# Two edits at the head of a fused DeltaNet and SwiGLU kernel: the first square roots move from GpSimd to VectorE, and the gate of the first weight loads moves behind a second pair of norms

## The chip, the cores and the metric

The kernel runs on one core of one Trainium2 chip. The time is that of the device, in microseconds (us), and the figure compared is the median of several runs. TensorE (PE) multiplies matrices and loads its weights in separate records (PEld), VectorE (DVE) and ScalarE (ACT) work on vectors, GpSimd (POOL) does some small work and issues a few transfers, and SyncE (SP) does nothing but issue transfers, in order. The instructions of each engine run in the order in which they were written; engines meet through semaphores.

## What is computed

The first half is a DeltaNet attention over 4 batches, 8 heads, 768 steps and 48 channels. The second is a SwiGLU block on 3072 tokens with 384 features and 1536 hidden units.

```python
k_n = k / (np.linalg.norm(k, axis=-1, keepdims=True) + 1e-06)
for t in range(S):
    y[:, :, t] = einsum('bhd,bhde->bhe', q[:, :, t], state)
    v_old = einsum('bhde,bhd->bhe', state, kt)
    state = state + bt[..., None, None] * einsum('bhd,bhe->bhde', kt, vt - v_old)
x = y.transpose(0, 2, 1, 3).reshape(B * S, H * D)
g = x @ w_gate
out = (g / (1 + exp(-g)) * (x @ w_val)) @ w_out
```

The change concerns `np.linalg.norm` of the first 128 steps: its square root.

## The kernel before, in words

The 768 steps are cut into 12 chunks of 64. A chunk holds all 32 pairs of batch and head at once; two chunks make a group, and for each group the recurrence inside a chunk is solved as a triangular system. Chunk by chunk, `advance` (four steps) turns the solved system and the running state into the tokens of the SwiGLU block, `x_ffn`. From then on TensorE does the large products `p_gate` and `p_val` (`gate_val`, L825) and `p_o`, and the attention of later chunks is fitted between them. The order of every engine is written out by hand, since the schedule is a manual one.

The head of the program, before the first `p_gate`, runs so:

- SP issues half of k for chunks 0 and 1 (`load_k`, L119; ACT issues the other half), then half of the beta loads (`load_beta`, L355; POOL issues the other half). Next come the first four pieces of the feed-forward weights (`stage`, L232), q of chunk 0 (`load_q`, L127), k of chunks 2 and 3, weight pieces 4 to 9, v of chunk 0 (`load_v`, L167), q of chunk 1, weight pieces 10 to 16, v of chunk 1, and q of chunk 2. They stand in one queue.
- The first weight piece is written into the buffer `places[0]`, whose first column DVE clears with a `memset` (L1128). The piece overwrites that column, so SP may not issue it before the `memset`. Everything behind it on SP waits too. In the kernel before, the `memset` stands between the norms of chunk 0 and those of chunk 1.
- `norms(c)` squares k on DVE (L331), sums the squares in three reductions (L339), and GpSimd then takes the square root with `pow` and an exponent of 0.5 (L343), 16 values in each partition for each of the two chunks.
- PE transposes k of chunks 0 and 1 (L410), forms the products of k with itself (`first_gram`, L524 and L525), and `first_diag` (L530) copies their diagonal blocks out, half of them by ACT and half by DVE. `first_n` (L364 to L368) adds the epsilon, takes the reciprocal and transposes it; `first_scale` (L543 to L546) scales beta on POOL and the matrix `mb` on DVE; `substitute` (L488, L494) solves the system of 32 columns on DVE in 62 dependent instructions.
- Meanwhile PE, in its order, transposes q of chunk 0 and k of chunks 2 and 3, forms their products (L422), transposes the matrices of the second group (`turned_m`, L566) and q of chunk 1 (L410). Only then does `join_late` for chunk 0 follow (L598, L608), which joins the halves of the solved system. It needs the result of `substitute` through `late_z` (L574, L580) and the ACT copies `d_o` (L591). Its result `zt` is copied by ACT (L616); then come `p_u` (L741), `p_y` (L760), the transposes `p_f` (L805), `x_ffn` (L808) and the first `p_gate` (L825).

The square roots of the later groups (`invert`, L633) stay on GpSimd in both kernels. The tile `n_t[0]` holds the 32 sums, later the norms, of the first group; `first_n` reads it, and ACT reads it in `scale_v_heads` (L374).

Of the kernel before, what the change touches and what calls it, by code (L numbers as in the profile page):

```python
# [8 lines left out]
FP32 = mybir.dt.float32  # L9
U32 = mybir.dt.uint32  # L10
ALU = mybir.AluOpType
# [4 lines left out]
R = 32  # L16
# [4 lines left out]
def kernel(  # L21
# [25 lines left out]
    nc = tc.nc  # L47
# [10 lines left out]
    HH = NB * H  # L58
# [4 lines left out]
    work = ctx.enter_context(tc.tile_pool(name="work", bufs=2))  # L63
# [60 lines left out]
    def load_q(c):  # L124
        for bp in range(NB):
            for b in range(2):
                nc.sync.dma_start(  # L127
                    out=qpad[c % QB][64 * b : 64 * b + 64, bp, :, 0:D],
                    in_=halves(q, c, bp, b).rearrange("h p d -> p h d"),
                )  # L130
# [59 lines left out]
    def words(tile_):  # L190
        return tile_.bitcast(U32)
# [95 lines left out]
    half = const.tile([128, R], FP32, name="half")  # L287
# [7 lines left out]
    for b in range(2):  # L295
        rows = mask_q[64 * b : 64 * b + 64]
        nc.gpsimd.affine_select(
            out=rows,
# [13 lines left out]
    def half_of(x):  # L312
        return slice(64 * x, 64 * x + 64)
# [7 lines left out]
    n_t = {}  # L321

    def new_n(g):

        n_t[g] = work.tile([128, 2, HH], FP32, name="n_t")

    def norms(c):

        ksq = work.tile([128, NB, H, D], FP32, name="ksq", tag="r", bufs=2)
        x = knp[c][:, :, :, 0:D]  # L330
        nc.vector.tensor_tensor(out=ksq, in0=x, in1=x, op=ALU.mult)  # L331
        n = n_t[0][:, c].rearrange("p (par bp j) -> p par bp j", par=2, bp=NB)
        ksq_v = ksq.rearrange("p bp (j par) d -> p par bp j d", par=2)
        for to, of, par in (
            (slice(0, 128), slice(0, 128), 0),
            (half_of(0), half_of(1), 1),
            (half_of(1), half_of(0), 1),
        ):
            nc.vector.tensor_reduce(  # L339
                out=n[to, par], in_=ksq_v[of, par], axis=mybir.AxisListType.X, op=ALU.add  # L340
            )
        n = n_t[0][:, c]
        nc.gpsimd.tensor_tensor(out=n, in0=n, in1=half[:, 0:HH], op=ALU.pow)  # L343

    def divide_beta(g, r_n):
        for _ in range(2):
# [4 lines left out]
    def load_beta(at, queue=nc.gpsimd):  # L351

        s_, blk, c, par = at // 8, at // 4 % 2, at // 2 % 2, at % 2
        lo, m = 64 * c + R * blk, (NG - 1) * 128 + R
        queue.dma_start(  # L355
            out=beta_s[8 * at : 8 * at + 8, 0:m],
            in_=beta.rearrange("(bp b) (j par) s -> b par bp j s", b=2, par=2)[
                s_ ^ par, par, :, :, lo : lo + m
            ],
        )  # L360

    def first_n():
        n = n_t[0].rearrange("p c h -> p (c h)")
        nc.vector.tensor_scalar_add(n, n, 1e-6)  # L364
        r_n = work.tile([128, R], FP32, name="r_n", tag="n_b", bufs=1)
        nc.vector.reciprocal(r_n, n)
        r_b = work.tile([128, R], FP32, name="r_b", tag="nb", bufs=1)
        nc.vector.transpose(r_b, r_n)  # L368
        return r_b
# [78 lines left out]
    def gram(*args):  # L448
        for _ in gram_steps(*args):
            pass  # L450
# [13 lines left out]
    def new_mb():  # L464
        return work.tile([128, R, R], FP32, name="mb", bufs=1)
# [39 lines left out]
    def first_tiles():  # L505
        a = work.tile([128, C * 2 * HH], FP32, name="a_sb")

        first_of["flat"] = a[:, 0 : R * R]
        first_of["diag"] = a[:, 0 : R * R].rearrange("p (j h) -> p h j", j=R)
        a_sb[0] = a[:, R * R :].rearrange("p (c h j) -> p c h j", c=2, h=HH)  # L510
        zb = work.tile([128, R, R], FP32, name="zb", bufs=1)
        nc.vector.memset(zb, 0.0)
        nc.vector.memset(ztp[0], 0.0)
        first_of["zb"] = zb
# [13 lines left out]
    def first_diag(c, par, p, copy):  # L528
        at = HH * c + HH // 2 * par
        copy(first_of["diag"][:, at : at + HH // 2], p[1][:, par, 1])  # L530
# [581 lines left out]
    with tc.manual_schedule(  # L1112
        engines={
            mybir.EngineType.PE,
            mybir.EngineType.Activation,
            mybir.EngineType.DVE,
            mybir.EngineType.SP,
            mybir.EngineType.Pool,
        }
    ):  # L1120
        new_n(0)
        for at in range(0, 16, 2):
            load_beta(at)
            load_beta(at + 1, nc.sync)
        first_tiles()
        norms(0)

        nc.vector.memset(places[0][:, 0:1], 0)  # L1128
        norms(1)
        for n in range(4):  # L1130
            stage(n)
        load_q(0)
        load_k(2)
        load_k(3)
        for n in range(4, 10):
            stage(n)
        load_v(0)
        load_q(1)
        stage(10)
        stage(11)  # L1140
        copy_a, copy_v = nc.scalar.copy, nc.vector.tensor_copy
        turned(0, False)
        turned(1, False, "py")
        p_g = [first_gram(0, "px"), first_gram(1, "py")]
        first_diag(0, 0, p_g[0], copy_a)
        first_diag(0, 1, p_g[0], copy_v)
        copy_a(beta_b, beta_s.rearrange("p (g r) -> p g r", g=NG)[:, :, 0:R])
        first_diag(1, 0, p_g[1], copy_a)
        r_b = first_n()
        first_diag(1, 1, p_g[1], copy_v)  # L1150
        mb = new_mb()
        nc.vector.transpose(
            mb.rearrange("p j i -> p (j i)"), first_of["flat"]
        )
        for n in range(12, 17):
            stage(n)
        load_v(1)
        zb = first_scale(mb, r_b)
        for c in range(2):
            first_below(c, p_g[c])  # L1160

        turned(0, True, "ffn")
        turned(2, False, "px")
        turned(3, False, "py")
        first_q = gram_steps(0, True, "ffn")
        next(first_q)
        gram(2, False, "px", (copy_a, copy_a))
        gram(3, False, "py", (copy_a, copy_a))
        for n, _ in enumerate(substitute(mb, zb)):
            if n == R // 2:  # L1170
                for i in range(4):
                    power_step(i)
        m_1 = turned_m(1, "ffn")
        scale_v_heads(0)
        turned(1, True, "px")
        for _ in late_z(0, zb):
            pass
        mb = new_mb()
        mbs.append(mb)
        first_join = join_late(0, 0, ("px", "py"))  # L1180
        next(first_join)
        converts(2)
        next(first_q)
        next(first_join)
        nc.scalar.copy(mb[:, m_1[0][0]], m_1[0][1])
        step("advance", advance, 0)
        converts(2)
        step("advance", advance, 0)
        nc.scalar.copy(mb[:, m_1[1][0]], m_1[1][1])
        converts(2)  # L1190
        step("advance", advance, 0)
        converts(2)
        step("advance", advance, 0)
        converts(2)
        second_inverse.append(invert(1))
        for _ in range(2):
            next(second_inverse[0])
        second = join_late(0, 1, ("ffn", "py"))
        converts(2)

        def state_and_join():
            step("advance", advance, 0)
            next(second)

        def second_join():
            next(second)
            gens["join", (0,)] = [None, 2]

        first.extend((state_and_join, second_join, lambda: gram(1, True)))


        pairs = [(c, f) for c in range(2) for f in range(0, 8, 2)]
        pairs += [(c, f) for f in range(8, FT, 2) for c in range(2)]
        for c, f in pairs:
            early = c == 0 and f < 8
            if c == 1 and f == 0:
                finish(1)
            elif f > 0:
                point(1 if early else 2)
            need((6, 12, 18, 18, 24, 24)[f // 2])  # L1220
            gate_val(c, f, fill, 1 if early else None)
        need(len(pieces))
        for bp in range(NB):
            point(2)
            output(0, bp, fill, (4, 8))
        output(1, 0, fill, (4, 8))
        hold.clear()
        first_blocks(True)
        first_blocks(False)
        point(2)  # L1230
        output(1, 1, fill, range(2, FT, 2))
        finish(2)
        for c in range(2, NCH):
            for f in range(0, FT, 2):
                point(c + 1)
                gate_val(c, f, fill)
            point(c + 1)
            if c >= FAST:
                output_fast(c, fill)
            else:  # L1240
                output(c, 0, fill)
                point(c + 1)
                output(c, 1, fill)
            finish(c + 1)
# [30 lines left out]
```

## Time and profile before

| what | value |
|---|---|
| median of 5 runs | 736.95 us (736.53 to 738.5) |
| the profiled execution | 737.05 us, its span 735.1 us |
| PE busy in the span | 697.8 us (95%) |
| DVE busy | 447.7 us (61%) |
| ACT busy | 167.5 us (23%) |
| POOL busy | 54.3 us (7%) |
| PE busy from 0 to 16, 16 to 32, 32 to 48, 48 to 64 us | 7.99, 10.95, 8.62, 9.04 us |
| first `p_gate` starts at | 63.24 us |

A row of a timeline gives the start in us, the time to the end of the last merged instruction, the engine (PEld for weight loads, a q behind the name for the part that issues transfers), the line, the operation, output and inputs by tile, and how many instructions are merged. The bracket tells how long the engine was idle before, and what ended the idleness; "issue" stands where the profile shows nothing that the engine waited for. The table of stretches gives the busy time of each engine in a stretch, the granted TensorE clock (PEclk) as a share of full speed, and the mean busy share of the 16 DMA engines.

### The profile page before, as it was taken

Reading aid. Unit: us, or ns where it says so; the run is one execution under the profiler, and the core shown is the slowest. Engines: PE = TensorE matmul, PEld = TensorE weight load, DVE = VectorE, ACT = ScalarE, POOL = GpSimd, SP = SyncE. Lnnn points to the kernel's source line nnn. Section 1 sums busy time; section 2 is a strip of 40 time slices with the busy share of each in tenths; the row PEclk is TensorE's granted clock in tenths of the full one; section 3 lists DMA queues with packets and bytes.
Section 4 is the critical chain, followed back from the end, with each engine's and each line's share of the span. In section 5 each row is a group of like instructions: output and inputs, shape, how many; then the busy total and the mean of one; then the engine's idle time right before and its main releaser. Section 6 shows DMA issues by size and latency. Waiting matters only on the chain.

```text
span 735.1 us, 22491 instructions
## 1 busy us (share of the span) xinstructions
PE 697.8 (95%) x10132; PEld 604.9 (82%) x10132; DVE 447.7 (61%) x904; ACT 167.5 (23%) x323; POOL 54.3 (7%) x46
## 2 busy tenths in 40 slices
PE   4757999999999999999999999999999999999997
PEld 3546898856787789988988988988988988989987
DVE  6995766687598163768853678853678853313122
ACT  3567754202401202021012021012011012021010
POOL 7003000203000000030000030000030000000000
PEclk9556999999999999999999999999999999999999
DMA  7786354210231112321302331302211100000100
GB/s 151 169 228 171 111 129 125 34 30 17 56 45 25 23 23 45 55 56 19 48 3 46 42 67 22 48 3 44 46 25 16 29 3 3 22 3 0 23 1 21
DMA packets 130736, 37.19 MB, mean 51 GB/s; under 512 B 122864, under 2 KB 125936, under 8 KB 130640
## 3 DMA queue, kind: packets, MB, share of 16 engines
q1 hardware_dynamic: 127184, 34.01, 22.9%
q10 hardware_dynamic: 3072, 1.57, 1.0%
q8 instruction: 79, 1.29, 0.7%
q0 software_dynamic: 384, 0.17, 0.1%
q14 instruction: 17, 0.14, 0.1%
HBM read 31.01 MB, written 4.72 MB: 49 GB/s over the span
## 4 chain that ended last, share of the span: by engine, by line
PE 82%; DVE 7%; DMA 3%; SPq 3%; ACT 2%; issue 1%; ACTq 0%; DVEq 0%
PE p_gate L825 24%; PE p_val L825 23%; PE p_o L937 15%; PE p_o L854 6%; PE p_g L422 2%; DVE tmp L488 2%; PE p_r L720 2%; PE p_u L741 2%; PE p_s L772 1%; PE p_y L760 1%; PE p_y L729 1%; DMA zt<-in_moe_w_gate_dram 1%; DVE zb L494 1%; SPq L127 1%; SPq L119 1%
## 5 line engine op out<-in xcount | busy, mean ns | idle before, releaser
L825 PE MATMUL p_gate<-x_ffn,wg_sb 128*128 128x256 f32 x864 | 204.8, 387 | 1.3 <-ACT x_ffn L808 1.3
L825 PE MATMUL p_val<-x_ffn,wv_sb 128*128 128x256 f32 x864 | 198.5, 379 | 0.0
L825 PEld LDWEIGHTS p_val<-x_ffn,wv_sb 128*128 128x128 f32 x864 | 163.8, 190 | 22.3
L825 PEld LDWEIGHTS p_gate<-x_ffn,wg_sb 128*128 128x128 f32 x864 | 161.3, 191 | 24.2 <-ACT x_ffn L808 1.8
L840 DVE TENSOR_TENSOR h_f<-sil,p_val 128x512 f32<-128x512 f32 x71 | 48.6, 684 | 162.8 <-PE p_val L825 162.6
L834 ACT ACTIVATE sil<-p_gate 128x512 f32<-128x512 f32 x72 | 43.0, 597 | 292.3 <-PE p_gate L825 270.6
L937 PE MATMUL p_o<-wo_sb,h_f 128*128 128x192 f32 x432 | 75.6, 328 | 0.1
L937 PEld LDWEIGHTS p_o<-wo_sb,h_f 128*128 128x128 f32 x432 | 70.3, 190 | 1.2 <-DVE o_sb L947 0.7
L488 DVE TENSOR_TENSOR tmp<-zb,mb 128x31 f32<-128x31 f32 (+15 forms) x186 | 63.3, 341 | 12.0 <-PE p_j L608 6.7
L494 DVE TENSOR_TENSOR zb<-zb,tmp 128x31 f32<-128x31 f32 (+15 forms) x186 | 63.8, 343 | 6.4
L633 POOL TENSOR_TENSOR n_b<-mb,half 128x32 f32<-128x32 f32 x5 | 30.4, 6085 | 409.8 <-DVE mb L458 369.6
L947 DVE TENSOR_TENSOR o_sb<-o_sb,p_o 128x192 f32<-128x192 f32 x45 | 15.8, 351 | 53.7 <-PE p_o L937 36.5
L854 PE MATMUL p_o<-wo_sb,h_f 128*128 128x384 f32 x136 | 45.7, 490 | 0.0
L854 PEld LDWEIGHTS p_o<-wo_sb,h_f 128*128 128x128 f32 x136 | 25.3, 190 | 16.5
L937 PE MATMUL p_o<-last_k,h_f 128*128 128x192 f32 x180 | 32.2, 326 | 0.0
L937 PEld LDWEIGHTS p_o<-last_k,h_f 128*128 128x128 f32 x180 | 29.7, 190 | 0.0
L895 DVE TENSOR_TENSOR h_f<-h_f,h_f 128x256 f32<-128x256 f32 x54 | 22.4, 424 | 8.0 <-PE p_o L937 7.1
L937 PE MATMUL p_o<-last_h,h_f 128*128 128x192 f32 x144 | 26.3, 326 | 0.0
L937 PEld LDWEIGHTS p_o<-last_h,h_f 128*128 128x128 f32 x144 | 23.9, 190 | 0.0
L741 PEld LDWEIGHTS p_u<-vin,zt 64*64 64x64 f32 x768 | 13.7, 141 | 5.6 <-issue 3.2
L458 DVE STREAM_TRANSPOSE mb<-a_sb 32x1024 f32<-32x1024 f32 x8 | 17.1, 2138 | 0.2
L752 ACT COPY uu<-p_u 128x768 f32<-128x768 f32 (+1 forms) x13 | 9.6, 749 | 31.7 <-PE p_u L741 31.7
(180 smaller groups left out, 682.9 us busy)
## 6 DMA issues: line engine op xcount, KB each, us to landing
vin<-in_v_dram SPq DMA_DIRECT2D x96, 48.0 KB
kn<-in_k_dram SPq DMA_DIRECT2D x40, 96.0 KB
out_dram<-o_sb SPq DMA_DIRECT2D x36, 96.0 KB
zt<-in_moe_w_out_dram SPq DMA_DIRECT2D x6, 384.0 KB
staged<-in_moe_w_out_dram SPq DMA_DIRECT2D x6, 384.0 KB
qpad<-in_q_dram SPq DMA_DIRECT2D x36, 64.0 KB
wo_sb<-in_moe_w_gate_dram SPq DMA_DIRECT2D x4, 512.0 KB
wo_sb<-in_moe_w_val_dram SPq DMA_DIRECT2D x4, 512.0 KB
```

What stands on the lines that cost most here:

```text
L458: nc.vector.transpose(out(rows, 0), in_(rows, 0))
L488: nc.vector.tensor_tensor(out=t_v, in0=zb[:, 0 : j + 1, j : j + 1].to_broadcast([128, j + 1, m]), in1=mb[:, j : j + 1, j + 1 : R].to_broad ...
L494: nc.vector.tensor_tensor(out=zb[:, 0 : j + 1, j + 1 : R], in0=zb[:, 0 : j + 1, j + 1 : R], in1=t_v, op=ALU.add,)
L633: nc.gpsimd.tensor_tensor(out=n, in0=mb.rearrange("p j i -> p (j i)")[:, 0 : R * R : R + 1], in1=half, op=ALU.pow,)
L741: nc.tensor.matmul(p_u[half_of(b), par, bp, j], zt[half_of(b ^ par), par, bp, j], r[half_of(b ^ par), par, bp, j], start=first, stop=True, ...
L825: nc.tensor.matmul(ps[name][:, i], w_sb[:, t, (f + i) * 128 : (f + i + 1) * 128], xts[c][:, t], start=(t == 0), stop=(t == KT - 1),)
L834: nc.scalar.activation(sil, ps[name], ACTF.Silu)
L840: nc.vector.tensor_tensor(out=hs[c, f], in0=sil, in1=ps["p_val"], op=ALU.mult)
L854: nc.tensor.matmul(p_o, hs[c, f - f % 2][:, f % 2, bp * 128 : (bp + 1) * 128], wo_sb[:, f], start=(f == 0), stop=(f == FT - 1),)
L895: nc.vector.tensor_tensor(out=out, in0=a, in1=b, op=ALU.subtract)
L937: nc.tensor.matmul(p[x, part], a(f - f % 2)[:, f % 2], b(f), start=not begun and f == 0, stop=f == FH - 1, skip_group_check=True,)
L947: nc.vector.tensor_tensor(out=out, in0=a, in1=b, op=ALU.add)
```

## The change

Three edits at the head of the program. `norms` ends with the reductions: the GpSimd `pow` of L343, two instructions of 128x16, is gone. The `memset` that holds back the first weight piece stands behind `norms(1)` instead of in front of it. A new function `first_roots`, called after the first copy of `first_diag`, takes the 32 roots on VectorE: a first guess of the inverse root from the bits of the number, three Newton steps, and a product with the number itself. That is 12 dependent instructions of 128x32. The tiles `x` and `t` take the places of tags that `first_n` uses right after them. All other instructions of all engines, those of SP included, keep their order.

```diff
@@ norms
-        n = n_t[0][:, c]
-        nc.gpsimd.tensor_tensor(out=n, in0=n, in1=half[:, 0:HH], op=ALU.pow)
@@ new
+    def first_roots():
+        n = n_t[0].rearrange("p c h -> p (c h)")
+        x = work.tile([128, R], FP32, name="x", tag="n_b", bufs=1)
+        t = work.tile([128, R], FP32, name="t", tag="nb", bufs=1)
+        nc.vector.tensor_scalar(
+            out=words(t), in0=words(n), scalar1=1, scalar2=None,
+            op0=ALU.logical_shift_right,
+        )
+        nc.vector.tensor_scalar(
+            out=words(x), in0=words(t), scalar1=-1.0, scalar2=float(0x5F3759DF),
+            op0=ALU.mult, op1=ALU.add,
+        )
+        for _ in range(3):
+            nc.vector.scalar_tensor_tensor(
+                out=t, in0=x, scalar=-0.5, in1=x, op0=ALU.mult, op1=ALU.mult
+            )
+            nc.vector.tensor_tensor(out=t, in0=t, in1=n, op=ALU.mult)
+            nc.vector.scalar_tensor_tensor(
+                out=x, in0=t, scalar=1.5, in1=x, op0=ALU.add, op1=ALU.mult
+            )
+        nc.vector.tensor_tensor(out=n, in0=n, in1=x, op=ALU.mult)
@@ the order of the head
         first_tiles()
         norms(0)
-
-        nc.vector.memset(places[0][:, 0:1], 0)
         norms(1)
+        nc.vector.memset(places[0][:, 0:1], 0)
         for n in range(4):
             stage(n)
...
         first_diag(0, 0, p_g[0], copy_a)
+        first_roots()
         first_diag(0, 1, p_g[0], copy_v)
```

## The prediction, made before the changed kernel was run

> **What bounds the kernel now.** I read the page first, then the chain of waits of the first 66 us, then the timelines of the engines over that stretch, last the transfers in narrow windows. The page says where a change at the head can count at all:
>
> ```profile
> span 735.1 us, 22491 instructions
> PE 697.8 (95%) x10132; PEld 604.9 (82%) x10132; DVE 447.7 (61%) x904; ACT 167.5 (23%) x323; POOL 54.3 (7%) x46
> PE   4757999999999999999999999999999999999997
> PEclk9556999999999999999999999999999999999999
> q8 instruction: 79, 1.29, 0.7%
> ```
>
> PE is the bound from the fifth slice (about 74 us) on. Before that it has holes, and whatever moves the first `p_gate` (63.24 us) moves the end by about as much. From there to 79 us the chain of waits runs through `p_gate`, a row of ACT conversions and the second join, all of which follow `x_ffn`; after 79.21 us it is PE alone. So the question is what sets `x_ffn`. SP and DVE at the start:
>
> ```profile
> 9.76 0.38 SPq L232 DMA_DIRECT2D h_f<-in_moe_w_gate_dram  x1
> 11.61 3.23 SPq L127 DMA_DIRECT2D qpad<-in_q_dram  x4
> 14.89 4.06 SPq L119 DMA_DIRECT2D kn<-in_k_dram  x4
> 19.00 2.67 SPq L119 DMA_DIRECT2D last_k<-in_k_dram  x4
> ...
> 9.94 1.68 DVE L339 TENSOR_REDUCE n_t<-ksq 128x8 f32<-128x384 f32 x3
> 12.70 0.59 DVE L530 COPY a_sb<-p_g 128x256 f32<-128x256 f32 x1 [1.09 <-ACT a_sb L530]
> 15.61 0.18 DVE L364 TENSOR_SCALAR n_t<-n_t 128x32 f32<-128x32 f32 x1 [2.32 <-POOL n_t L343]
> ```
>
> SP issues without a pause from 0.81 to 37.7 us; its queue carries q, k, v and weights alike, so a wait on it delays all of them. DVE stands 2.32 us before `first_n`, waiting for GpSimd's `pow`. That is the wait the first edit removes. Now PE:
>
> ```profile
> 15.03 0.19 PE L524 MATMUL p_g<-kt 64*32 64x32 f32 x1 [2.09 <-issue]
> ...
> 31.83 0.47 PE L422 MATMUL p_g<-last_k 64*64 64x64 f32 x17 [1.59 <-issue]
> 33.49 1.80 PE L566 MATMUL p_m<-ident,a_sb 32*32 32x32 f32 x111 [1.19 <-ACT a_sb L445]
> 35.84 2.05 PE L566 MATMUL p_m<-ident,a_sb 32*32 32x32 f32 x128 [0.54 <-issue]
> 41.48 0.45 PE L566 MATMUL p_m<-ident,a_sb 32*32 32x32 f32 x17 [3.60 <-issue]
> 45.20 1.08 PE L598 MATMUL p_j<-zt,a_sb 32*32 32x32 f32 x64 [1.36 <-DVE zt L574]
> ...
> 50.42 0.26 PE L608 MATMUL p_j<-ident,d_o 32*32 32x32 f32 x2 [2.22 <-issue]
> ```
>
> Idle "issue" time with no releaser ends at 15.03, 31.83, 35.84, 41.48 and 50.42 us, and between the later ends lie 128 matmuls each (17 + 111, then 128). On the page the instruction queue q8 moved 79 packets; 20,264 PE and PEld records over 79 make 256, which is 128 matmuls with their loads. The packets of q8 start at 12.81, 29.19, 33.03, 38.95 and 47.79 us, take 0.95 to 1.32 us each, and PE goes on 1.27 to 1.46 us after each has ended. I read these gaps as PE out of instructions until the next packet has come. The last gap matters: ACT's scaled copy that the rest of `p_j` needs ended at 47.88 us, but PE stood until 50.42, and `zt`, `p_u`, `p_y` and `x_ffn` follow one on the other from there. DVE's chain (`substitute` ends at 43.07, its two transposes at 46.15 us) is thus covered by some 2.2 us. The packet of 47.79 us starts just as the weight and v transfers that SP issued from 34.8 us on run dry: DMA share 0.99, 1.00 and 0.97 in the stretches 36 to 40, 40 to 44 and 44 to 48 us, then 0.43.
>
> **The change part by part.** *Pow removed.* Two GpSimd instructions, 6.59 us from 8.98 to 15.57. Nothing else on POOL waits behind them but the beta products at 16.57.
>
> *Roots added.* 12 dependent instructions of 128x32 on DVE. The trace of before has dependent instructions of 128x31 (first steps of `substitute`), 0.19 us each and 0.22 from start to start: 12 x 0.22 = 2.6 us. The nearest rows bound it: `nb` with 0.14 + 0.03 gives 2.0, the reciprocal with 0.35 + 0.04 gives 4.7. The first is an arithmetic instruction of the same kind and width as the Newton steps, so I take 2.6. They begin after the reductions (11.62) and the memset (0.06), at about 11.7, and end at 14.3. Behind them on DVE wait the copy of L530 (0.62, to 14.9) and `first_n` (0.81, to 15.75 instead of 16.42). ACT's later diagonal copy waits for that DVE copy too, and before it ran only at 15.81, after PE. DVE gains 0 (if PE's second gram still ends at 15.8, because the next DVE copy needs ACT's, 15.81 to 16.40) to 0.65 us (if it comes earlier). By either end the gain goes into the cover of 2.2 us: the end gets 0. If the cover went, it would be part of the rival below.
>
> [...]
>
> *Memset moved.* SP was free for the first weight piece at 9.76 us. Now it waits for the memset behind `norms(1)`: 11.62 + 0.06 and some 0.05 until SP goes, 11.73. That is +1.97 us. Queued behind the waiting issue on SP are all of q0, k2, k3, weights 4 to 9, v0, q1, weights 10 to 16, v1 and q2; no other queue is crossed, and POOL's beta transfers are issued by then (7.93). SP was never idle after 9.76 in the head, so nothing there takes the delay up, unless issues that took longer than their kind (four rows of q and k at 1.17, 1.41, 1.25 and 1.82 us, where the others take 0.63 to 0.66) become short. The first three are 1.9 us together, made while the first weights were moving; the weights now move just as much before the same issues, so I take none back. Bounds: +0.1 (all three given back) to +2.1 us.
>
> Who waits for it: PE's transposes of q0 and k2, k3 stood for these transfers (1.81 before 17.59, put down to POOL, whose clearing of that tile was long done; 0.90 before 21.48; 0.57 before 24.63), so PE moves by 1.97 too; the weights and v that fill the DMA engines from 36 us also; and with both the instruction packets that lie between them. The packet of 47.79 starts at 49.76, PE goes on at 52.39, `x_ffn` and the first `p_gate` come 1.97 us later, at 65.21. I take this value since every step on the path was led by SP's order; less would need PE and the weights to move against each other.
>
> *Clock.* Granted clock was 0.50 from 33.1 to 67.2 us and 1.00 in the stretch after; the first `p_gate` took 4.82 us for 12 matmuls, later ones 2.79 to 2.59. The changes of clock stand on a grid of 3.413 us (12.6, 16.0, 29.7, 33.1, 67.2), and the stretch before each rise was filled by PE. On this same grid a `p_gate` from 65.21 would be slow to 70.6, 12 matmuls at 0.465 us, 5.58 us: +0.76. With the grid elsewhere it is -0.32 (only 3.41 us slow) to +0.76; I take 0, the page's execution being close to the median, and keep both ends.
>
> The Trainium skill, "TensorE: Matmul & The Clock Gate", section on the clock gate, says that the window is free-running and not reset when a kernel starts. One profile cannot show that; by the rule the mean over all phases is an estimate of +0.4 us, beside the 0 used.
>
> *Sum.* 737.05 (own time: span 735.10 and 1.95 around it) + 1.97 + 0 = 739.0 us. The profiled execution lies 0.1 above the median, so the median should be **738.9 us**. About 0.2%, 1.5 us (735.5 to 738.4), is what a measurement here can tell from no change; this is just outside.
>
> **Rivals.**
>
> *The last packet comes earlier (ends faster).* One mechanism: the gap before 50.42 shrinks. The packet of 38.95 us came 3.1 us after PE had passed the boundary before it, because transfers stood in its way from 36.2 on, and PE then stood 3.60 us; the next one, 6.3 us after the boundary at 41.48. Should PE reach 35.84's boundary about 1 us earlier against SP's queue (its second gram may end a microsecond sooner, with the packet of 12.81 no longer beside weights), both packets slip ahead of the big transfers. Then the join is led by q1's transposes (45.81), ACT's copies (46.97), `p_j` (48.13), and 128 matmuls of L608 (95 took 1.5 us, so 2.0): `zt` starts at 50.25, not 51.98. Time: 737.05 - 1.7 - 0.1 = 735.2. It decides once that packet starts before 47.8 us; below 45.5 all of it is won. Against it: PE waits for q0, k2 and k3 in between, all on SP, which takes the head start away again.
>
> *SP makes up for part, or the delay is hidden.* The long issues turn short: +0.1 to +1.4 us, 737.0 to 738.3. For it: they coincide with the first weights in flight. Against it: the 1.82 us issue at 32.95 has a DMA share of only 0.5 around it, so length doesn't need a load.
>
> *The change does what it says.* DVE's 0.65 us reach the end and transfers have slack: 736.3. Against it stands the 2.2 us cover, and the Trainium skill speaks for it: "Runtime: NRT & Kernel Launch", section on instruction fetch mechanics, holds that fetches are mostly hidden. The rows of 1.59 to 3.60 us above differ from that page.
>
> **How the numbers follow.** Forecast 0.58, at 738.3 to 740.4 (0.5 us of slack in SP below, the clock's 0.76 and 0.1 in the memset above, with the runs' own spread). Made up in part 0.17; does what it says 0.10; earlier packet 0.15. Range 736.0 to 740.6, which leaves out the earlier packet and little above. Chances: faster by over 0.2% is the earlier packet less its weak outcomes, 0.14; within 0.2%, the two middle rivals and a little of the others, 0.27; slower 0.59.
>
> **What the changed profile would show.** Right: the first weight issue on SP near 11.73; q0's near 13.6; 12 DVE rows of about 0.19 us in 2.6 us, no POOL row before `first_n`; the issue gap of `p_j` still there, ending near 52.4; `x_ffn` near 64.7. Wrong: that gap under 1 us, or SP's q1 issues back at 31 to 33 us. Most of all I would be wrong if PE's packets and the weights move against each other, which no row of before can exclude.

## The result, and the profile after

The changed kernel takes 737.94 us (median of 31 runs, 736.49 to 741.67), the kernel before 736.76 us (52 runs, 734.99 to 739.21). The ratio is 1.0017 with the interval 1.0011 to 1.0023, at 736.8 us some 1.25 us longer, 0.8 to 1.7. That is slower, and it lies inside the 0.2% that I had set as the bound of "no change". The forecast of 738.9 us had the sign and overstated the size: +1.95 us instead of +1.25.

The profiled execution of the changed kernel took 736.93 us, 1.0 below its own median, and that of before 737.05 us. These two pages therefore cannot be subtracted to find the 1.25 us; single executions of one kernel differ by about as much. They show the order of the work, and the times are taken from the medians. In one execution of the experiment `q_first` TensorE was slow throughout (2471.88 us, a matmul of `p_val` 1112 ns on average, where `q_first_look`, the same kernel, has 379), and it is left out of the comparisons.

The page after:

```profile
span 735.1 us, 22500 instructions
PE 696.8 (95%) x10132; PEld 604.1 (82%) x10132; DVE 449.6 (61%) x916; ACT 167.4 (23%) x323; POOL 47.8 (6%) x44
PE   4657999999999999999999999999999999999997
q8 instruction: 79, 1.29, 0.7%
```

GpSimd has lost 6.5 us of busy time and two instructions, VectorE has gained 12 instructions and 1.9 us. The 79 instruction packets are as they were, and of PE's slices only the second differs (6 where it was 7). SP's timeline (start, time until the end of the last merged issue):

```profile
11.43 0.37 SPq L232 DMA_DIRECT2D h_f<-in_moe_w_gate_dram  x1
11.85 1.17 SPq L232 DMA_DIRECT2D h_f<-in_moe_w_val_dram  x1
...
14.01 2.69 SPq L127 DMA_DIRECT2D qpad<-in_q_dram  x4
16.75 3.96 SPq L119 DMA_DIRECT2D kn<-in_k_dram  x4
20.75 2.68 SPq L119 DMA_DIRECT2D last_k<-in_k_dram  x4
...
32.55 3.40 SPq L127 DMA_DIRECT2D qpad<-in_q_dram  x4
...
36.66 0.43 SPq L232 DMA_DIRECT2D zt<-in_moe_w_val_dram  x1
```

The first weight issue stands 1.67 us later than in the profile before (9.76), q0 by 2.40, k3 by 1.75, q1 by 1.62 (30.93). The last row is weight piece 11; in the profile before it was

```profile
35.49 0.43 SPq L232 DMA_DIRECT2D zt<-in_moe_w_val_dram  x1
```

so it is only 1.17 us later: SP has taken back part of the delay on the way. DVE's timeline of the changed kernel:

```profile
9.61 1.68 DVE L339 TENSOR_REDUCE n_t<-ksq 128x8 f32<-128x384 f32 x3
11.32 0.18 DVE L365 TENSOR_SCALAR t<-n_t 128x32 uint32<-128x32 uint32 x1
11.35 0.06 DVE L1149 MEMSET h_f<- 128x1 uint32 x1
...
13.78 0.19 DVE L381 TENSOR_TENSOR n_t<-n_t,x 128x32 f32<-128x32 f32 x1
13.89 0.60 DVE L551 COPY a_sb<-p_g 128x256 f32<-128x256 f32 x1
14.33 0.18 DVE L385 TENSOR_SCALAR n_t<-n_t 128x32 f32<-128x32 f32 x1
15.54 0.59 DVE L551 COPY a_sb<-p_g 128x256 f32<-128x256 f32 x1 [0.40 <-ACT a_sb L551]
16.17 1.25 DVE L1173 STREAM_TRANSPOSE mb<-a_sb 128x1024 f32<-128x1024 f32 x1
```

The twelve roots run from 11.32 to 13.97, 2.65 us. `first_n` (L385) no longer waits for POOL. What ends DVE's last idle time here is ACT's diagonal copy, 0.40 us, and the transpose of `mb` begins at 16.17 (17.06 before): in this execution DVE did gain 0.9 us. PE, and ACT's copy of q1, from the timeline:

```profile
14.14 0.19 PE L545 MATMUL p_g<-kt 64*32 64x32 f32 x1 [1.54 <-issue]
...
40.71 0.46 PE L587 MATMUL p_m<-ident,a_sb 32*32 32x32 f32 x17 [2.50 <-issue]
43.16 1.07 ACT L433 COPY qt<-p_t 128x512 f32<-128x512 f32 x2 [3.19 <-PE p_t L431]
44.32 1.08 PE L619 MATMUL p_j<-zt,a_sb 32*32 32x32 f32 x64 [1.25 <-ACT qt L433]
50.09 0.26 PE L629 MATMUL p_j<-ident,d_o 32*32 32x32 f32 x2 [2.77 <-issue]
...
62.91 4.80 PE L846 MATMUL p_gate<-x_ffn,wg_sb 128*128 128x256 f32 x12 [0.95 <-ACT x_ffn L829]
```

DVE's 0.9 us arrive at `p_j`, which starts at 44.32 instead of 45.20. (Its row names ACT's copy of q1, which ends at 44.23, level with DVE's transpose of `zt`, 44.18.) Then they are gone: PE runs out of instructions as before and stands 2.77 us instead of 2.22, and resumes at 50.09 instead of 50.42. The packet that ends this gap starts at 47.03 (47.79 before). The stretches of that time show why not earlier (us, busy us of PE, PEld, DVE, ACT and POOL, granted clock, DMA share, GB/s):

```profile
40.00:44.00 4.00, 2.36 (x25) 1.89 (x24) 3.69 (x10) 0.84 (x2) 0.00 (x0) 0.50 1.01 379
44.00:48.00 4.00, 2.32 (x101) 1.88 (x102) 4.00 (x10) 2.85 (x7) 0.00 (x0) 0.50 1.09 311
48.00:52.00 4.00, 1.49 (x91) 1.35 (x90) 4.00 (x16) 2.08 (x7) 0.00 (x0) 0.50 0.42 73
```

The 16 DMA engines are full until 48 us with the weights and v behind SP's late issues. The packet starts in the last microsecond of the weights, of which the last transfer starts at 47.6; before, it started 0.6 us after the last one (47.2).

### The profile page after: what moved, and what is told of

Read it like the earlier page. It is cut to its first block, busy times and chain, and to the rows that moved or that the text cites. A ratio compares the mean times of both kernels' runs of the same rounds, so it can differ in the third digit from the quotient of the medians.

```text
span 735.1 us, 22500 instructions
## 1 busy us (share of the span) xinstructions
PE 696.8 (95%) x10132; PEld 604.1 (82%) x10132; DVE 449.6 (61%) x916; ACT 167.4 (23%) x323; POOL 47.8 (6%) x44
## 4 chain that ended last, share of the span: by engine, by line
PE 76%; DVE 16%; issue 3%; ACT 3%; DMA 1%; POOL 1%; SPq 0%; DVEq 0%; ACTq 0%
PE p_gate L846 24%; PE p_val L846 23%; PE p_o L958 14%; DVE tmp L509 5%; DVE zb L515 4%; PE p_g L443 2%; PE p_o L875 2%; PE p_u L762 1%; PE p_r L741 1%; PE p_s L793 1%; PE p_y L781 1%; PE p_y L750 1%; DVE h_f L916 1%; POOL n_b L654 1%; PE p_f L826 1%
```

## The experiments

The quoted expectations name their theories by letters; below each I say in words which of their numbers held. Microseconds of a ratio are taken at 736.8 us; the runs of before that a kernel is compared with were made on the same chip. Each kernel computes the whole reference.

### Each edit by itself

`gate_only` has only the moved memset, on the kernel before (`pow` stays):

```diff
         norms(0)
-        nc.vector.memset(places[0][:, 0:1], 0)
         norms(1)
+        nc.vector.memset(places[0][:, 0:1], 0)
```

> The clear of the first weight buffer behind norms(1), as in the changed kernel; the square roots stay on GpSimd. Theory A (SP's wait is the price: its first weight issue goes from 9.76 to about 11.5 us, and q, k, weights and v behind it all come later): +1.3 us against the kernel before (+0.8 to +1.9), the same as the whole change. Rival B (the roots on VectorE are the price, the gate is hidden): 0 (-0.3 to +0.3). Rival C (the two edits together do it, each alone nothing): 0.

`roots_only` has only the roots: the memset goes back between the norms.

```diff
         norms(0)
+        nc.vector.memset(places[0][:, 0:1], 0)
         norms(1)
-        nc.vector.memset(places[0][:, 0:1], 0)
```

> The square roots on VectorE, the clear of the first weight buffer where it was before. Theory A: the 0.65 to 0.9 us that VectorE gains lies under PE's wait for instructions at the join, so 0 (-0.5 to +0.2) against the kernel before, and SP's first weight issue at about 9.7 us again. Rival B: +1.3 us, as the whole change.

`gate_only`: 737.47 beside 736.42 us, 1.0012 (1.0003 to 1.0021), +0.9 us (0.2 to 1.5). `roots_only`: 737.28, 1.0007 (0.9996 to 1.0019), +0.5 us (-0.3 to +1.4). The moved memset alone costs time, whatever takes the roots; its own band of +0.8 to +1.9 holds the +0.9. The roots alone gain nothing that the median shows; a loss is not excluded, and the +1.3 of the theory that they are the price lies just inside the interval. How the 1.25 us divide between the two edits is thus known only to some 0.8 us. DVE's timeline of `roots_only` shows where their gain stops:

```profile
16.10 0.59 DVE L551 COPY a_sb<-p_g 128x256 f32<-128x256 f32 x1 [0.65 <-ACT a_sb L551]
16.73 1.25 DVE L1173 STREAM_TRANSPOSE mb<-a_sb 128x1024 f32<-128x1024 f32 x1
```

With the weights early again, the packet for PE's second gram starts at 12.26 (11.39 in the changed kernel), ACT's diagonal copy follows late, and DVE stands 0.65 us for it: the wait for POOL has become one for PE's instructions. Of before, the two single edits and the changed kernel only the last, with both, has `mb` at 16.17. The profiled execution of `roots_only` took 735.09 us, 2.2 below its own median, and its first `p_gate` starts at 61.60, 1.6 earlier than in the profile before; the median does not bear this out.

### Does VectorE lead? Twice the Newton steps

```diff
-        for _ in range(3):
+        for _ in range(6):
```

> The changed kernel with six Newton steps in place of three: 9 more dependent instructions on VectorE, 9 x 0.225 = 2.0 us, ahead of the substitution; SP's order and times are untouched. Theory A (VectorE's chain has 2.2 to 2.8 us to spare at the join): as the changed kernel, +1.3 us against the kernel before (+0.9 to +1.8), and the wait of p_j with the reason issue shrinks from 2.77 to under 1 us. Rival D (VectorE's chain sets the first x_ffn): +3.3 us (+2.8 to +3.6).

738.58 beside 736.42 us, 1.0023 (1.0011 to 1.0035): +1.7 us (0.8 to 2.6). Nine more instructions, 2.0 us on DVE, cost some 0.5 over the changed kernel, which the intervals do not tell from nothing. The +1.3 of the theory that DVE is covered holds, the +3.3 of the theory that DVE leads lies outside. PE's timeline:

```profile
46.55 0.97 PE L619 MATMUL p_j<-zt,a_sb 32*32 32x32 f32 x56 [1.22 <-ACT qt L433]
50.71 0.26 PE L629 MATMUL p_j<-ident,d_o 32*32 32x32 f32 x2 [1.40 <-issue]
```

`p_j` starts 2.2 us later than in the changed kernel and its issue gap shrinks from 2.77 to 1.40 us, so PE goes on only 0.6 us later. I had expected the gap below 1 us. The gap takes in the delay, but it does not go to zero. In this execution DVE is not alone in being late: its transpose of `zt` ends at 46.16, and ACT's copy of q1, which `p_j` waited for, at 46.49.

### Is the loss SP's? The whole block behind the roots

`gate_late` moves the memset and all SP issues from the first weight piece up to piece 11 behind `first_roots`:

```diff
         norms(1)
-        nc.vector.memset(places[0][:, 0:1], 0)
-        for n in range(4):
-            stage(n)
-        load_q(0)
...
-        stage(11)
...
         first_roots()
+        nc.vector.memset(places[0][:, 0:1], 0)
+        for n in range(4):
+            stage(n)
+        load_q(0)
...
+        stage(11)
```

> The changed kernel with the clear of the first weight buffer, and so the same SP issues in the same order behind it, placed after the roots: SP's first weight issue at about 14 us in place of 11.43 (2.5 us more) and 9.76 in the kernel before. Theory A (SP's wait reaches the end nearly one for one): +3.0 to +4.0 us against the kernel before, so 1.8 to 2.7 above the changed kernel. Rival F (the wait is mostly hidden by waits of SP for earlier transfers and by VectorE's chain, and 1.25 us is a threshold effect): +1.0 to +2.0 us.

739.51 beside 736.69 us, 1.0042 (1.0029 to 1.0055): +3.1 us (2.1 to 4.1). The time follows SP's start, as the theory of +3.0 to +4.0 has it; the +1 to +2 of the other falls. SP's timeline:

```profile
14.32 0.38 SPq L232 DMA_DIRECT2D h_f<-in_moe_w_gate_dram  x1
...
15.23 1.75 SPq L232 DMA_DIRECT2D h_f<-in_moe_w_gate_dram  x1
...
17.50 2.69 SPq L127 DMA_DIRECT2D qpad<-in_q_dram  x4
...
39.05 0.43 SPq L232 DMA_DIRECT2D zt<-in_moe_w_val_dram  x1
```

With this the size of the effect can be read. I measure from the start of the last three beta issues, which stand ahead of the gate in every kernel:

| SP after its beta issues, us | first weight issue | weight piece 11 | time against before |
|---|---|---|---|
| early gate: before, `before_look`, `roots_only` | 2.05, 2.04, 2.05 | 27.78, 27.84, 27.20 | |
| memset behind `norms(1)`: after, `gate_only`, `newton6` | 3.82, 4.07, 4.16 | 29.05, 29.25, 28.91 | +1.25, +0.9, +1.7 |
| `gate_late` | 6.72 | 31.45 | +3.1 |

The mean delay of the first issue is 1.97 and 4.67 us; at piece 11, 1.46 and 3.84 us are left. SP takes back 0.5 and 0.8 us. It stands in the rows: q0's four issues took 3.23, 3.41 and 2.99 us with the early gate and 2.69 with each later one, and those of k2 4.06, 4.23 and 4.36 us against 3.96, 3.37 and 3.71 behind `norms(1)` and 2.95 in `gate_late`. Against this, one of the first weight issues takes 1.17 to 1.75 instead of 0.43. The time goes up by about 0.65 us for each microsecond of SP's wait (1.25 of 1.97, 3.1 of 4.67; 0.4 to 0.9 by the two intervals). In `gate_late` the chain that carries it is in plain sight in PE's and ACT's timelines:

```profile
45.65 0.45 PE L587 MATMUL p_m<-ident,a_sb 32*32 32x32 f32 x17 [3.60 <-issue]
49.22 0.95 PE L619 MATMUL p_j<-zt,a_sb 32*32 32x32 f32 x53 [1.22 <-ACT qt L433]
53.60 0.26 PE L629 MATMUL p_j<-ident,d_o 32*32 32x32 f32 x2 [2.40 <-issue]
```

```profile
48.09 1.07 ACT L433 COPY qt<-p_t 128x512 f32<-128x512 f32 x2 [4.81 <-PE p_t L431]
```

DVE's transposes had ended at 45.58. PE stood 3.60 us for the packet that lets it finish `p_m`, then transposed q1, ACT copied it at 48.09, and `p_j` began after that. So at this dose DVE, 3.6 us early, is not the leader; the packets and q1's chain are.

### Do the weights stand in the packet's way?

`q_first` puts q0, k2 and k3 ahead of the first four weight pieces; `q_first_look` is the same kernel.

```diff
-        for n in range(4):
-            stage(n)
         load_q(0)
         load_k(2)
         load_k(3)
+        for n in range(4):
+            stage(n)
```

> The changed kernel with the loads of q of chunk 0 and k of chunks 2 and 3 issued ahead of weight pieces 0 to 3 instead of behind them, so that the clear delays nothing (SP comes to the first weight piece only at about 17.5 us). Same bytes, same work. Theory A (PE's chain of q, k, instruction packets and q of chunk 1 is led by SP's order): PE's transposes of q0 start near 14.5 instead of 17.6 to 19.9 us, the packet of 47 to 48 us starts before 44, the wait of p_j under 1 us, x_ffn 1.5 to 2.2 us earlier than before, time -1.8 us against the kernel before (-2.5 to -0.8). Rival E (what counts is how late the weights come, which here are 7.7 us later than in the kernel before for pieces 0 to 3): slower than the kernel before by 1.3 us or more.

> The same kernel as q_first, for a profile of an execution at full TensorE speed, which the first did not give. Theory A as it stood for q_first: packet of 47 us before 44, wait of p_j under 1 us, x_ffn 1.5 to 2.2 us earlier than in the kernel before. Since q_first's time came out at +0.1%, the profile should show either that this gain is there and lost behind x_ffn (late weights: waits of ACT or VectorE for pieces 0 to 9 or 12 to 16), or that the packet still comes at 47 us.

737.48 beside 736.42 us, 1.0010 (1.0001 to 1.0019), and 737.43 beside 736.69, 1.0007 (0.9998 to 1.0016): +0.5 to +0.7 us, where I expected 1.8 us less than before. The +1.3 or more of the rival theory is inside the first interval only at its edge and outside the second. PE's timeline and two stretches of the second:

```profile
37.14 0.46 PE L587 MATMUL p_m<-ident,a_sb 32*32 32x32 f32 x17 [1.68 <-issue]
44.19 1.08 PE L619 MATMUL p_j<-zt,a_sb 32*32 32x32 f32 x64 [4.69 <-DVE zt L595]
50.51 0.26 PE L629 MATMUL p_j<-ident,d_o 32*32 32x32 f32 x2 [3.31 <-issue]
```

```profile
40.00:44.00 4.00, 0.00 (x0) 0.00 (x0) 3.73 (x10) 0.67 (x2) 0.00 (x0) 0.50 0.94 339
44.00:48.00 4.00, 2.32 (x101) 1.88 (x102) 4.00 (x11) 2.75 (x7) 0.00 (x0) 0.50 1.10 362
```

PE resumed `p_m` 3.6 us earlier than in the changed kernel and stood idle from 39.5 to 44.2 us, yet the packet started only at 47.55. An earlier PE does not bring the packet ahead of the weights: for that, PE would have to get into `p_j`, and `p_j` waits for DVE.

The next two take the weights away instead. `late10` drops pieces 10 to 16 from the head and lets SP issue them behind v1 and q2, gated by a memset at step 27 of `substitute`; `late_join` gates them behind the first conversions after `p_j` has begun.

```diff
-        stage(10)
-        stage(11)
...
-        for n in range(12, 17):
-            stage(n)
         for n, _ in enumerate(substitute(mb, zb)):
+            if n == 27:
+                nc.vector.memset(places["wo"][:, 8 * H_ : 8 * H_ + 1], 0)
+                for i in range(10, 17):
+                    stage(i)
```

> The changed kernel with weight pieces 10 to 16 issued behind v of chunk 1 and held back by a clear on VectorE at step 27 of the substitution (about 41 us) in place of 36 to 40 us. Their first use on ACT is at 57 us. Theory A (PE's waits at 40.71 and 50.09 us are instruction packets standing behind these transfers): the packets of 38.34 and 47.03 us start by 37.5 and 43 us, the wait of p_j goes under 0.7 us, zt's copy starts near 49.3 in place of 51.65, time -2.0 us against the changed kernel, -0.8 (-1.5 to +0.2) against the kernel before. Rival G (the packets come late for another reason, or the weights are needed where they were): no gain, +1.2 us or more against the kernel before.

```diff
-        stage(10)
-        stage(11)
...
-        for n in range(12, 17):
-            stage(n)
...
         next(first_join)
+        held = freed_by.pop(0, [])
         converts(2)
+        nc.vector.memset(places["wo"][:, 8 * H_ : 8 * H_ + 1], 0)
+        for i in [*range(10, 17), *held]:
+            stage(i)
```

> The changed kernel with weight pieces 10 to 16 held back until VectorE has converted pieces 0 and 1 (about 47 us), issued behind v1 and q2, and the one piece that the first conversion frees behind them. Theory H, from the runs so far: PE asks for the packet that ends p_j's wait only when p_j itself begins (44 to 46 us), it needs 3.3 us from there at least and more where large transfers stand in its way, and the time is the start of zt's copy plus 685.3 us on average. Then the packet of 47 us starts by 46.2, PE goes on by 48.6, the next packet starts by 50 (late10: 51.94, and 1.51 us lost in p_u), zt's copy starts near 49.8: time -1.6 us against the kernel before (-2.2 to -0.6). Rival I (what late10 lost was not the second packet, or late weights cost behind x_ffn): as late10, +0.3 us (-0.3 to +0.9).

`late10`: 737.25 beside 736.69 us, 1.0005 (0.9996 to 1.0013), +0.4 us (-0.3 to +1.0), between the -0.8 that I expected and the +1.2 of the rival theory. `late_join`: 737.47 beside 736.9, 1.0002 (0.9991 to 1.0013), +0.1 us (-0.7 to +1.0), where I expected -1.6; the rival theory, "as `late10`", holds. PE's timeline of `late10`, then its stretches:

```profile
44.86 0.95 PE L619 MATMUL p_j<-zt,a_sb 32*32 32x32 f32 x53 [1.22 <-ACT qt L433]
48.16 0.26 PE L629 MATMUL p_j<-ident,d_o 32*32 32x32 f32 x2 [0.85 <-issue]
...
54.36 1.09 PE L762 MATMUL p_u<-vin,zt 64*64 64x48 f32 x27 [1.23 <-issue]
```

```profile
40.00:44.00 4.00, 2.36 (x25) 1.89 (x24) 3.70 (x11) 0.84 (x4) 0.00 (x0) 0.50 0.31 52
44.00:48.00 4.00, 2.07 (x101) 1.68 (x102) 4.00 (x10) 3.45 (x9) 0.00 (x0) 0.50 0.79 165
52.00:56.00 4.00, 2.07 (x52) 1.85 (x52) 3.33 (x11) 2.51 (x8) 0.00 (x0) 0.50 1.01 404
```

Two things follow. With no weights in the way the packet still did not start before `p_j` had: 45.87, 1.0 us after it; but then PE resumed 1.9 us earlier than in the changed kernel. (The share of 0.79 in that stretch is v and q; in `best`, below, the engines were idle from 45 to 46 us, and the packet also came 1.0 us after `p_j`.) I read this as the weights standing in its way, and PE's own progress setting the earliest time. And the gain was given back: the weights now fill the engines from about 49 us, the next packet (51.94) goes among them, and a gap of 1.23 us that was not there before opens in `p_u`. `late_join` shows the same gap of 1.23 us (ending at 55.01).

Over all profiles but that of `q_first` the packet that ends the gap of `p_j` starts as follows (us; the fourth column is the start of the last weight transfer of the stretch up to 52 us, "none" where the weights came only behind the packet):

| kernel | `p_j` starts | packet starts | last weight transfer | PE resumes | `p_gate` |
|---|---|---|---|---|---|
| before | 45.20 | 47.79 | 47.2 | 50.42 | 63.24 |
| `before_look` | 46.43 | 47.12 | 47.4 | 49.80 | 62.61 |
| after | 44.32 | 47.03 | 47.6 | 50.09 | 62.91 |
| `gate_only` | 44.76 | 47.32 | 47.3 | 49.98 | 62.80 |
| `roots_only` | 45.72 | 46.47 | 48.4 | 48.78 | 61.60 |
| `newton6` | 46.55 | 47.66 | 47.3 | 50.71 | 63.53 |
| `gate_late` | 49.22 | 50.75 | 51.8 | 53.60 | 66.42 |
| `q_first_look` | 44.19 | 47.55 | 47.9 | 50.51 | 63.34 |
| `late10` | 44.86 | 45.87 | none | 48.16 | 62.54 |
| `late_join` | 45.06 | 46.50 | none | 48.81 | 63.17 |
| `best` | 45.55 | 46.53 | none | 48.85 | 62.12 |
| `best_pow` | 45.35 | 46.26 | none | 48.66 | 61.95 |
| `best_gate` | 44.23 | 45.19 | none | 48.09 | 61.09 |

The packet never starts before `p_j`. Beside the weights it starts near their end but not always behind the last of them: in `roots_only` it went 1.9 us ahead of it, when the DMA share had fallen to 0.32 (46 to 47 us).

The Trainium skill, "Runtime: NRT & Kernel Launch", section on instruction fetch mechanics, says that an engine's instructions come in blocks of 256 and that the next block is fetched while the current one runs, mostly hidden. The blocks agree with these traces, but the fetch is not hidden in this stretch, where 128 small matmuls with their loads last about 2 us and the packet starts late.

### Versions that might gain

`best` joins `late_join` and `q_first`. `best_pow` makes the same two edits on the kernel before, with `pow` and the early memset, and so asks what the drawn change is worth where the packets are out of the way. `best_gate` adds to `best` a memset that holds q0 behind `norms(1)`, so that PE's first packet has no transfer beside it:

```diff
         nc.vector.memset(places[0][:, 0:1], 0)
+        nc.vector.memset(qpad[0][:, 0, 0, 0:1], 0.0)
         load_q(0)
```

> late_join and q_first together: q0, k2, k3 ahead of weight pieces 0 to 3, pieces 10 to 16 held back to about 47 us. Theory H: p_j begins when VectorE's transposes are through, at 44.1, since ACT's copies of q1 end by 41; packet of p_j by 45.3, PE on by 47.6, zt's copy near 49.1: -2.3 us against the kernel before (-3.0 to -1.2), 0.3 to 1.0 us below late_join. Rival J (q_first showed no gain, so the order of q and k does not matter): as late_join.

> As best, but with the square roots on GpSimd and the clear of the first buffer where they were in the kernel before. The roots alone are tested where nothing covers VectorE's chain. Theory H: p_j begins 0.65 to 0.9 us later than in best, so +0.7 us against best (+0.3 to +1.0), near -1.6 us against the kernel before. Rival B' (the roots on VectorE gain nothing at any place, since ACT's copy of the second diagonal block leads): within 0.2 us of best.

> best, with the first load of q0 held back behind norms(1) by a clear of one column, as the changed kernel holds back the first weight piece. In best the first instruction packet of PE started at 12.57 us beside q0's transfers, PE's second gram ended near 16.1, and VectorE waited 1.43 us for ACT's copy of it, so the roots gained nothing. Theory K (the gate's use is that this packet comes at 11.4 to 11.9 us): the wait of 1.43 us falls to about 0.4, VectorE's transpose of mb starts near 16.2 in place of 17.44, its last transposes 1.0 to 1.3 us earlier, ACT's d_o and with it zt's copy as much: -1.0 us against best, -1.6 us against the kernel before (-2.4 to -0.8). SP's 1.7 us of waiting cost nothing, since ACT's copies of q1 end 4 us or more before p_j begins. Rival L (the gain is lost again between VectorE and zt, or the wait of SP costs as much as it did in the changed kernel): as best or slower, -0.7 us or worse against the kernel before.

`best`: 736.01 beside 736.9 us, 0.9991 (0.9982 to 1.0001), -0.7 us (-1.3 to +0.1), where I expected -2.3. `best_pow`: 736.15, 0.9989 (0.9980 to 0.9999), -0.8 us (-1.5 to -0.1): the only version whose interval lies below 1, and it leaves out the whole change studied here. The two do not differ, so the roots gain nothing there either, and the theory that they give 0.7 us falls. DVE's timeline of `best` names the reason:

```profile
16.80 0.60 DVE L551 COPY a_sb<-p_g 128x256 f32<-128x256 f32 x1 [1.43 <-ACT a_sb L551]
17.44 1.25 DVE L1171 STREAM_TRANSPOSE mb<-a_sb 128x1024 f32<-128x1024 f32 x1
```

q0 now went out at once, PE's first packet started at 12.57 beside it, ACT's diagonal copy came at 16.17, and DVE stood 1.43 us. That is what `best_gate` mends, and in its profiled execution it did so at every step. PE's timeline:

```profile
44.23 1.08 PE L619 MATMUL p_j<-zt,a_sb 32*32 32x32 f32 x64 [2.33 <-DVE zt L595]
...
48.09 0.26 PE L629 MATMUL p_j<-ident,d_o 32*32 32x32 f32 x2 [0.85 <-issue]
```

The transpose of `mb` began at 16.11, and `p_gate` at 61.09. That execution took 734.96 us; but the median is 736.44 beside 736.51, 1.0000 (0.9991 to 1.0009), where I expected -1.6. Why the median does not follow is open.

### A second execution of the kernel before

> The kernel before, unchanged, for a second profile: how far the start of x_ffn and the wait of p_j vary from execution to execution. Expected, if the wait of p_j is set by transfers that run beside it: first p_gate 62 to 64 us, wait 0.9 to 2.8 us, and the sum from the first p_gate to the end within 0.7 us of 671.9 us.

One execution without any edit, 738.51 us. PE goes on with `p_j` at 49.80 and the first `p_gate` starts at 62.61, 0.6 earlier than in the first profile, though the execution took 1.5 us longer; it has a stretch of 3.4 us at half clock near 190 us. From the first `p_gate` to the end of the span it took 674.0 us, outside the 671.2 to 672.6 that I expected. The head of one kernel thus varies by 0.6 us between two executions, and the rest by more. What leads `p_j` varies too. In the first profile it was DVE's transpose, here it is ACT's copy of q1, which stands on the path that SP's order leads:

```profile
46.43 0.95 PE L598 MATMUL p_j<-zt,a_sb 32*32 32x32 f32 x53 [1.22 <-ACT qt L412]
49.80 0.26 PE L608 MATMUL p_j<-ident,d_o 32*32 32x32 f32 x2 [1.13 <-issue]
```

## Why the prediction was right or wrong

- *Pow removed, roots added.* Right: twelve instructions of 0.18 to 0.19 us, 2.65 us predicted as 2.6. DVE's gain was taken as 0 to 0.65 us and was 0.9 in the profile after, by the start of `mb`; the roots alone gave 0.3 (`roots_only`, 16.73), the memset alone 0.4 (`gate_only`, 16.65). The second profile of before has 17.48, so the last two are no more than executions differ by. That no gain reaches the end is borne out by `roots_only` (+0.5, -0.3 to +1.4) and by `best` beside `best_pow`.
- *"By either end the gain goes into the cover of 2.2 us."* Right in effect, by another mechanism. The 2.2 us are not a fixed packet under which DVE has room: the packet starts only once PE has begun `p_j`, and beside the weights only near their end. In the profile after, DVE's gain goes into a longer gap (2.77 us); 2.0 us more on DVE cost about 0.5 (`newton6`). One reading of the lines was slightly off: after the packet of 33.03 PE goes on 1.48 us after its end, outside the "1.27 to 1.46".
- *Memset moved: SP's first issue +1.97.* Right: 1.97 us in the mean of three profiles each. "I take none back" is the step that failed. SP took back 0.5 us up to piece 11, in issues that I had named, those of q0 and k2, although the reason given against it ("the weights now move just as much") had them stay long: +1.46 us are left. The time rose by 1.25 us (0.8 to 1.7), and by 3.1 for 4.67. The term of 1.97 was mis-sized by 0.7 us; 0.5 of it are SP's, and the other 0.2 are below what these runs resolve.
- *"The packet of 47.79 starts at 49.76, PE goes on at 52.39", `p_gate` at 65.21.* Not seen in the profile after: 47.03, 50.09 and 62.91 in an execution 1.0 us below the median. `gate_late`, profiled within 0.3 us of its median, has 50.75, 53.60 and 66.42, so the chain named is shown at the larger dose. Where the 1.25 us sit in a median execution of the changed kernel stays open. Of the two signs of being wrong, the gap under 1 us did not come, but "q1 issues back at 31 to 33 us" did (32.55); that sign was badly chosen, since the forecast's own delay put them at 32.90.
- *Clock 0.* No run contradicts it. From `p_gate` to the first silu it took 4.28 to 5.53 us in these profiles, and the rise to full clock came anywhere from 64.4 to 69.6 us. That is a width of 1.25 us beside the 1.08 that I gave it.
- *Rivals.* The main forecast's own band, 738.3 to 740.4 us with a chance of 0.58, does not hold the 737.94. "SP makes up for part", with 0.17, named 737.0 to 738.3 us and does; its mechanism is shown for 0.5 us, so it was this rival and the forecast together. That the full range of 736.0 to 740.6 held the result owes something to its width, which took in three of the four cases. By its ratio the result is "within 0.2%", which had 0.27 against 0.59 for slower. "The last packet comes earlier" has its premise confirmed, since PE went on with the second gram earlier (14.14 against 15.03) with the packet of 12.81 moved to 11.39; yet the later packet started at 47.03, under the 47.8 from which it was to decide, and the end did not gain. "It does what it says" falls, with `roots_only`.

## What to carry to other kernels

An instruction taken out of a wait on one engine is worth what the last wait of its stage allows: look which releaser ends PE's idle time next, and whether that is a wait that moves with the work. The delay of a queue that carries all loads did reach the end here, at about 0.65 us for each microsecond; price it where the queue's last member stands, since issues that ran long beside transfers became short. Large transfers beside hundreds of tiny matmuls are worth a try at moving, but here the moved ones met the next such place, and the best version gained 0.8 us.

## What I had not expected of the hardware

- The packet that ends the gap of `p_j` started at the earliest 0.7 to 1.0 us after `p_j` had begun, even with the DMA engines idle (share 0.00 from 45 to 46 us in `best`), and PE went on 2.3 to 3.1 us after that. With the DMA engines full it started 2.6 to 3.4 us after `p_j` (before, after, `q_first_look`), and 1.1 and 1.5 us after it where `p_j` itself came late (`newton6`, `gate_late`). I read this as PE asking for a block only when it has nearly used up the one before.
- Executions of one kernel spread by about 4 us (52 runs of before: 734.99 to 739.21). Over these profiles the time from the first `p_gate` to the first silu, in which the clock rises, differs by up to 1.25 us. The Trainium skill, "TensorE: Matmul & The Clock Gate", section on the clock gate, calls the clock's window free-running; rises from 64.4 to 69.6 us, over first `p_gate`s from 61.09 to 66.42 us, agree with it.
- From the first silu to the end it took 667.1 to 667.4 us in all profiles but `before_look`, whatever was done to the head.
